# Linear attention followed by a spectral mix: the last attention step hands its weight tiles to the output phase, and y and z leave in one put

## The chip, the cores and the metric

The kernel runs on one core of one Trainium2 chip. The metric is device time in microseconds (us) from the first to the last instruction of that core. An execution of the kernel before takes 442.25 us (median of three: 441.34 to 443.05); the profiled one has a span of 441.4 us.

## The reference, cut to what matters

Shapes: q, k, v are 8 x 8 x 576 x 64 (batch, heads, sequence, head size), w_r and w_i are 64 x 512 x 512 (one matrix per frequency mode), w_ch is 512 x 512.

```python
def phi(x):
    proj = np.einsum('bhsd,df->bhsf', x, w_phi)
    proj = proj - np.max(np.abs(proj), axis=-1, keepdims=True)
    return np.concatenate([np.exp(proj), np.exp(-proj)], axis=-1)
q_p, k_p = phi(q), phi(k)
kv = np.einsum('bhsf,bhsd->bhfd', k_p, v);  z = np.sum(k_p, axis=2)
num = np.einsum('bhsf,bhfd->bhsd', q_p, kv)
den = np.einsum('bhsf,bhf->bhs', q_p, z)[..., None] + 1e-06
x = (num / den)                       # laid out as batch x sequence x 512
...
X = np.fft.rfft(x, axis=1)            # 64 lowest modes are mixed
Yr = Xr @ w_r - Xi @ w_i;  Yi = Xr @ w_i + Xi @ w_r      # per mode
y = np.fft.irfft(Y, n=S, axis=1)
u = x + y
out = u + np.maximum(u @ w_ch, 0.0)
```

The weights w_r and w_i are 134 MB in f32 and are read once. They are cast to bf16 on the way into SBUF.

## The kernel before, in words

**Two phases.** The attention phase works through 16 units (`Unit`, L101): one unit is a pair of heads (g, 4 of them) and a pair of batches (bp, 4 of them). A software pipeline (L504 to L573) runs steps n = -2 to 16; in each step one unit is finished (P: its x goes through the forward transform, `freq` and `keep_x`), one is in its second half (Q), one in its first (K), one is turned (R). In the last step, n = 16, there is only P, the last unit. The output phase (from L574) turns x into the result.

**The spectral mix.** The 64 modes form 8 octets (o = 0 to 7); each octet of a head pair g has a tile of w_r (even number) and one of w_i (odd number): key (g, 2 o + i). A tile is 1 MB in bf16, 8 KB on each of 128 partitions. `mix` (L461) takes one tile: eight matmuls into a PSUM bank `py`; after the second tile of an octet the bank is added to `yacc` (g < 3) or, for g = 3, becomes y of that octet. The keys are mixed in a fixed order (L351 to L354): all of g = 0 and 1, then g = 2 and 3 for octets 0 to 5, then octets 6 and 7 for g = 2 and 3 in turn. So (2,11) is the last of g = 2 for octet 5, (3,11) the tile that completes octet 5 over all g, and (3,15) the last of all.

**Loads.** `next_w` (L359) issues the next tile load from GpSimd's queue; one is issued after each mix. Tiles lie in nine buffers of pool `pw` (L83); six tiles of g = 0 lie in memory that is needed only later (`home`, L327; their keys are in `held`, L496). A load into a buffer waits until the tile before it in that buffer has been mixed.

**Who mixes when.** In the attention phase `some(n)` (L488) mixes up to n tiles at three or four places of a step: X = 3 a step from step 5 on (L506), also in step 16. The rest, 21 tiles, is mixed in the output phase's loop (L900). Instructions keep the order in which they are written on each engine (`InOrder`, L27).

**The output phase.** `todo` (L793) is a list of 76 tasks that are independent of the mixes that are still to come. The first 37 work on 36 chunks of x, 128 rows each: turn the chunk on TensorE, copy (VectorE), multiply with w_ch, keep the product in `xw` (ScalarE). The last three of these hold their product in PSUM. The other 39 tasks (`Absorb`, L724) add the inverse transform of octets 0 to 5 (for batches 0 and 1 also octet 6) to x and to xw: they read `yall` and `zall`, where z = y times w_ch. 42 tasks (A = 9 + K with K = 33, L795) are kept for the end: the three holds and the absorbs. In the loop, `n` tasks follow each mix (`fill`, L797); n is worked out from the number of mixes left (L912).

**y and z.** After the second tile of an octet with g = 3 (L913 to L953), y is rounded to `yst` (VectorE), turned, multiplied with w_ch (eight matmuls, 256 wide), and the product is rounded to `zst`. `yst` and `zst` have 128 partitions (mode, real or imaginary, batch) x 512; `put` (L802) stores each with a DMA from SyncE into 16 partitions of `yall` or `zall`, batch by batch in the free dimension: 128 packets of 1 KB, 128 KB. yall, zall and yl (late octets) are tiles of pool `pw`, so they take three of the nine tile buffers. Octets 6 and 7 also go to `yl`.

**The end.** After the last mix, 20 `Last` items (L811, L895 to L982) add the late octets, apply the relu and store.

Of the kernel before, what the change touches and what calls it, by code (L numbers as in the profile page):

```python
# [11 lines left out]
BF16 = mybir.dt.bfloat16  # L12
# [5 lines left out]
B_, H_, S_, D_ = 8, 8, 576, 64  # L18
NMODES = 64
DMODEL = 512  # L20
# [23 lines left out]
def kernel(  # L44
# [15 lines left out]
    pool, sp = InOrder(tc, nc.gpsimd), InOrder(tc, nc.sync)  # L60

    const = ctx.enter_context(tc.tile_pool(name="const", bufs=1))
    pers = ctx.enter_context(tc.tile_pool(name="pers", bufs=1))
# [13 lines left out]
    xflat = pers.tile([128, 16 + NG * NP * 18 * D_], BF16, name="xs")  # L77
    xs = xflat[:, 16:].rearrange("p (g b n d) -> p g b n d", g=NG, b=NP, n=18)
    yacc = pers.tile([128, NO, DMODEL], F32, name="yacc")

    XTb = [pers.tile([128, 2, 2, 2, 2, B_, 32], BF16, name=f"XT{i}") for i in range(2)]

    pw_cm = tc.tile_pool(name="pw", bufs=9)  # L83
    pw = pw_cm.__enter__()
    pin_cm = tc.tile_pool(name="pin", bufs=2)
    pin = pin_cm.__enter__()
# [14 lines left out]
    class Unit:  # L101
# [43 lines left out]
        def rows(self, tT, i, out):  # L145
# [7 lines left out]
            else:  # L153
# [3 lines left out]
            src = ps.rearrange("p (a c) f -> p a c f", a=2) if len(out.shape) == 3 else ps  # L157
            dve.tensor_reduce(out=out, in_=src, axis=AX.X, op=ALU.max,
                              apply_absolute_value=True)
# [167 lines left out]
    def home(g, w):  # L327

        if g == 0 and w in (0, 9):
            h = w // 9  # L330
            t = yacc.bitcast(BF16).rearrange("p o e -> p (o e)")[:, 4096 * h:4096 * h + 4096]
        elif g == 0 and w == 5:
            t = XTb[1].rearrange("p u r t x b m -> p (u r t x b m)")
        elif g == 0 and w in (3, 12, 13):
            t = xs[:, max(w - 10, 1)].rearrange("p b n d -> p (b n d)")[:, 0:4096]
        else:
            return pw.tile([128, 4, 2, DMODEL], BF16, name="wt", tag="wt")
        return t.rearrange("p (m r e) -> p m r e", m=4, r=2)
# [12 lines left out]
    wq = [(g, mg) for g in range(2) for mg in range(2 * NO)]  # L351
    wq += [(g, mg) for g in (2, 3) for mg in range(12)]
    wq += [(g, 2 * o + i) for o in (6, 7) for g in (2, 3) for i in range(2)]
    order = list(wq)  # L354
    wq.remove((0, 5))
    wq.insert(1, (0, 5))
    mixq = []

    def next_w(n):  # L359
        for _ in range(n):  # L360
            if wq:
                key = wq.pop(0)
                wts[key] = wload(*key)
# [65 lines left out]
    for t in range(3):  # L429
# [7 lines left out]
                      in_=every[:, 0:16].rearrange("p (a j c) -> p a c j", a=2, j=4),  # L437
                      axis=AX.X, op=ALU.add)
    dve.tensor_scalar_mul(out=minus[:, 0:4], in0=mf[0:96, 32:36], scalar1=-1.0)
# [48 lines left out]
    def some(n):  # L488
        for _ in range(n):
            if mixq:  # L490
                key = mixq.pop(0)
                mix(*key, wts.pop(key), XTb[key[0] % 2], lambda: one([128, DMODEL]))
                if key not in held:
                    next_w(1)

    held = [(0, mg) for mg in (0, 3, 5, 9, 12, 13)]  # L496
    units[1].load_k()
    units[1].load_v()
    units[1].load_q()
# [1 line left out]
    def unit(i):  # L501
        return units[i] if 0 <= i < len(units) else None

    for n in range(-2, len(units) + 1):  # L504
        P, Q, K, R = (unit(n + i) for i in (-1, 0, 1, 2))
        X = 0 if n < 4 else 6 if n == 4 else 3  # L506
        if Q:
            Q.exp_q(0)
        if K:
            K.rows_k(0)  # L510
            K.exp_k(0)
        if Q:
            Q.weigh_v2()
            if unit(n + 2):
                unit(n + 2).load_v()
        if P:
            P.freq()
            P.keep_x()
            if P.bp == NP - 1:
                mixq += [key for key in order if key[0] == P.g and (P.g < 2 or key[1] < 12)]  # L520
        if Q:
            Q.cols_q(1)
            Q.exp_q(1)
        some(1 if X else 0)
        if K:
            K.rows_k(1)
            K.exp_k(1)
        if Q:
            Q.kv()
        some(2 if n == 4 else 0)  # L530
        if K:
            K.rows_q(0)
            K.rows_k(2)
            K.rows_q(2)
            K.rows_q(1)
        if Q:
            Q.cols_q(2)
            Q.keep_kv()
            Q.exp_q(2)
        if K:  # L540
            K.exp_k(2)
            K.weigh_v()
        some(1 if X else 0)
        if R:
            R.turn_k(0)
        if K:
            K.shift_q()
        if R:
            R.turn_k(1)
        if Q:  # L550
            Q.num(0)
        if K:
            K.cols_q(0)
        if R and unit(n + 4):
            unit(n + 4).load_k()
        if Q:
            Q.num(6)
        if R:
            R.turn_q(0)
            R.turn_q(1)  # L560
            if unit(n + 4):
                unit(n + 4).load_q()
        if Q:
            Q.num(12)
        some(X - 2)
        if n == -1:
            forward_table()
        if n < 3:
            next_w((2, 3, 2, 3, 2)[n + 2])
        elif n == 3:  # L570
            next_w(1)
        if n == 6:
            pool.dma_start(wchb, moe_w_ch.rearrange("(dc p) e -> p dc e", p=128))  # L573
# [14 lines left out]
    pb_cm = tc.tile_pool(name="pb", bufs=2)  # L588
    pb = pb_cm.__enter__()
    xw = pb.tile([128, NP, 9, DMODEL], BF16, name="xw", bufs=1)  # L590
    zall = pw.tile([128, B_, DMODEL], BF16, name="zall", tag="wt")
    yall = pw.tile([128, B_, DMODEL], BF16, name="yall", tag="wt")
    yl = pw.tile([128, B_, DMODEL], BF16, name="yl", tag="wt")
    CI = pb.tile([128, 5, 128], BF16, name="CI", bufs=1)
    CL = pb.tile([128, 5, 128], BF16, name="CL", bufs=1)
# [83 lines left out]
    class Channels:  # L679
# [29 lines left out]
        def hold(self, pf):  # L709
            for g in range(NG):  # L710
                pe.matmul(pf, lhsT=self.xT[:, g, :], rhs=wchb[:, g, :],
                          start=(g == 0), stop=False)
# [80 lines left out]
    todo = [ch[0].turn] + [lambda i=i: hold(i) for i in range(len(ch))]  # L793
    todo += [c.only_x for c in ab[K:]] + [c.only_w for c in ab[K:]] + [c.all for c in full]
    A = 3 * 3 + K  # L795
# [3 lines left out]
            if todo:  # L799
                todo.pop(0)()  # L800

    def put(src, o, dst, copies):  # L802
        if o < 7:
            sp.dma_start(dst[16 * o:16 * o + 16], src)
        if o > 5:
            for s in copies:
                r = 32 * s + 16 * (o - 6)
                (pool if o == 6 else sp).dma_start(yl[r:r + 16], src)
# [91 lines left out]
    while mixq:  # L900
        key = mixq.pop(0)
        g, o, i = key[0], key[1] // 2, key[1] % 2
        if key not in wts:
            next_w(1)
        if not mixq:
            assert not todo
            seq[0].base(1)
            seq[0].base(0)
        mix(*key, wts.pop(key), XTb[g % 2], bank)
        next_w(1)  # L910
        left = len(mixq)
        n = -(-max(len(todo) - A, 0) // (left - 7)) if left > 7 else math.ceil(len(todo) / (left - 0.4)) if left else 0  # L912
        if g == NG - 1 and i == 1:  # L913
            end = left == 0
            if end:
                seq[1].base(1)
            py = pys.pop(o)
            yst = pb.tile([128, DMODEL], BF16, name="yst")
            pt = [bank([128, 2, 128], BF16) for h in range(2)]
            yT = [pb.tile([128, 2, 128], BF16, name=f"yT{h}") for h in range(2)]  # L920
            for h in range(2):
                dve.tensor_tensor(out=yst[:, H * h:H * h + H], in0=py[:, H * h:H * h + H],
                                  in1=yacc[:, o, H * h:H * h + H], op=ALU.add)
            put(yst, o, yall, (0, 2))
            if o < 5:
                fill(min(n, 1))
            for h in range(2):
                for dc in range(2):
                    pe.transpose(pt[h][:, dc, :],
                                 yst[:, H * h + 128 * dc:H * h + 128 * dc + 128], ident_b)  # L930
                if h:
                    dve.tensor_copy(yT[h], pt[h])
                else:
                    act.copy(yT[h], pt[h])
            if o < 5:
                fill(min(n - 1, 1))
            elif end:
                seq[0].straight(0)
                seq[0].keep_p()
                seq[1].base(0)  # L940
            pz = [bank([128, H]) for e in range(2)]
            for h in range(2):
                for e in range(2):
                    for dc in range(2):
                        pe.matmul(
                            pz[e], lhsT=yT[h][:, dc, :],
                            rhs=wchb[:, 2 * h + dc, H * e:H * e + H],
                            start=(h == dc == 0), stop=(h == dc == 1))
            zst = pb.tile([128, DMODEL], BF16, name="zst")
            act.copy(zst[:, 0:H], pz[0])  # L950
            dve.tensor_copy(zst[:, H:], pz[1])
            put(zst, o, zall, (1, 3))
            fill(max(n - 2, 0) if o < 5 else n)  # L953
        else:
            fill(n)
# [58 lines left out]
```

## Time and profile before

| what | from the profile of before |
|---|---|
| span | 441.4 us |
| TensorE (PE) busy | 330.6 us, 75% |
| VectorE (DVE) busy | 298.0 us, 68% |
| ScalarE (ACT) busy | 278.3 us, 63% |
| GpSimd (POOL) busy | 97.2 us, 22% |
| load queue q0 | 86.45 MB, its packets fill 99.6% of 16 engines' span |
| store queue q1 (SyncE) | 12.45 MB, 8.0% |
| weight loads on GpSimd's queue | 1024 KB each, 28.7 and 28.8 us from issue to landing (median) |
| puts into yall and zall | 7 each, 128 KB, 6.5 and 6.4 us from issue to landing (median) |
| granted TensorE clock, mean | 0.90 |

The profile's page has the busy time of each engine, then the span in 40 slices of 11 us each with the busy share in tenths (9 is 90% or more) and the DMA engines' share beside it. The chain of waits is followed back from the last instruction: each line is a start, a duration and what it was. A timeline line has start, duration, engine, line of the kernel, operation, the tiles written and read, a shape and a count, and in brackets the idle time just before it with what ended it. Nearly all instructions carry line L37, that of the helper that keeps the order, so one goes by tile names: `pt` and `one` are PSUM banks, `wt` a weight tile, `XT` the transformed x, `xs` is x, `xT` a turned chunk. "wt,XT" is a mix, "ident_b,xs" the turn of a chunk, "wchb,xT" its product with w_ch.

### The profile page before, as it was taken

The page shows a single profiled execution, that of the slowest core. Times are in us where ns is not written, and L with a number is a line of the kernel's source. Part 1 is how long each engine was busy: PE and PEld are TensorE (multiplying, and loading weights), DVE is VectorE, ACT ScalarE, POOL GpSimd, SP SyncE. Part 2 cuts the span into 40 slices and gives each one's busy share as a digit, 9 for nine tenths or more (in the row PEclk, how much of TensorE's full clock was granted, in tenths as well). Part 3 has the DMA queues.
Part 4 walks back from the last instruction along what each step waited for, and adds up shares of the span by engine and source line. Part 5 has one row for each costly group of instructions (what it writes and reads, how often), then busy time and mean ns, then how long its engine had stood idle before and what let it go on. Part 6 is the DMA issues. An engine that isn't in the chain of part 4 may idle for free.

```text
span 441.4 us, 10119 instructions
## 1 busy us (share of the span) xinstructions
PE 330.6 (75%) x4203; PEld 201.8 (46%) x4247; DVE 298.0 (68%) x583; ACT 278.3 (63%) x478; POOL 97.2 (22%) x138
## 2 busy tenths in 40 slices
PE   2577658768777787787786785926689979999992
PEld 2355546536555555455555453603345534344320
DVE  5768776776684777875877678717764333776694
ACT  3688877877797577865877766502644431656781
POOL 7232132132221222221122121211101220010171
PEclk9769987999899699885989799967999998999997
DMA  8999999999999999999999999999999999995787
GB/s 164 237 211 210 237 212 237 235 214 242 233 211 238 223 230 232 237 216 233 232 216 235 208 236 231 219 212 211 211 216 223 221 224 215 213 218 127 243 354 305
DMA packets 51582, 99.55 MB, mean 226 GB/s; under 512 B 2512, under 2 KB 13648, under 8 KB 51536
## 3 DMA queue, kind: packets, MB, share of 16 engines
q0 software_dynamic: 45376, 86.45, 99.6%
q1 hardware_dynamic: 6160, 12.45, 8.0%
q8 instruction: 33, 0.54, 0.5%
q14 instruction: 13, 0.11, 0.1%
HBM read 163.64 MB, written 9.44 MB: 392 GB/s over the span
## 4 chain that ended last, share of the span: by engine, by line
DMA 39%; PE 30%; DVE 12%; ACT 9%; issue 7%; POOL 0%; ACTq 0%; POOLq 0%; DVEq 0%
DMA vn<-in_v_dram 18%; PE one L37 11%; DMA wt<-in_moe_w_r_dram 9%; PE pt L37 9%; DMA wt<-in_moe_w_i_dram 6%; ACT AB L37 5%; PE pp L37 5%; PE two L37 5%; DMA kb<-in_k_dram 5%; DVE mk L37 3%; DVE m L37 2%; DVE xs L37 2%; DMA qb<-in_q_dram 2%; ACT AQ L37 1%; DVE va L37 1%
## 5 line engine op out<-in xcount | busy, mean ns | idle before, releaser
L37 ACT ACTIVATE AB<-two 128x1024 bf16<-128x1024 f32 x64 | 62.0, 1026 | 18.3 <-DVE mk L37 14.6
L37 ACT ACTIVATE AQ<-two 128x1024 bf16<-128x1024 f32 x64 | 62.6, 1045 | 2.6 <-PE two L37 2.5
L37 ACT CAST xw<-pt 128x512 bf16<-128x512 f32 x50 | 29.4, 588 | 46.3 <-PE pt L37 30.6
L37 DVE TENSOR_REDUCE m<-two 128x8 f32<-128x1024 f32 x32 | 39.2, 1224 | 15.3 <-PE two L37 15.2
L37 DVE TENSOR_TENSOR va<-vn,ee 128x1152 bf16<-128x1152 f32 x32 | 42.0, 1355 | 6.6 <-DMA vn<-in_v_dram 6.6
L37 DVE TENSOR_REDUCE mk<-two 128x8 f32<-128x1024 f32 x32 | 38.9, 1218 | 7.5 <-PE two L37 7.5
L37 PE MATMUL pt<-wchb,xT 128*128 128x512 bf16 x127 | 35.1, 389 | 8.1 <-DVE xT L37 6.3
L37 POOL DMA_DIRECT2D wt<-in_moe_w_i_dram x28 | 20.9, 748 | 87.2 <-PE pt L37 39.6
L37 POOL DMA_DIRECT2D wt<-in_moe_w_r_dram x30 | 22.4, 747 | 75.0 <-PE one L37 35.2
L37 PE MATMUL one<-wt,XT 128*32 128x512 bf16 x304 | 27.8, 451 | 13.9 <-DMA wt<-in_moe_w_i_dram 5.6
L37 PEld LDWEIGHTS <-xs 128*128 128x128 bf16 x624 | 31.6, 103 | 13.1 <-issue 8.0
L37 PE MATMUL two<-w2blk,qT 128*128 128x256 bf16 x128 | 22.8, 309 | 18.2 <-ACT AB L37 9.7
L37 ACT COPY qT<-one 128x512 bf16<-128x512 bf16 (+1 forms) x32 | 19.3, 641 | 26.2 <-PE one L37 25.8
L37 PEld LDWEIGHTS <-qT 128*128 128x128 bf16 x144 | 14.8, 107 | 36.6 <-issue 32.8
L37 PEld LDWEIGHTS <-XT 128*32 128x32 bf16 x512 | 14.4, 149 | 33.9 <-issue 18.8
L37 PE MATMUL two<-mT,minus 96*128 96x512 bf16 x64 | 27.1, 424 | 3.5 <-issue 1.5
L37 DVE TENSOR_TENSOR xs<-one,rd 128x384 bf16<-128x384 f32 x48 | 26.7, 557 | 1.6
L37 PEld LDWEIGHTS <-AQ 128*128 128x128 bf16 x512 | 24.2, 107 | 7.7 <-issue 3.9
L37 PE MATMUL one<-kvz,AQ 128*128 128x65 bf16 x512 | 26.9, 207 | 1.1 <-ACT qT L37 1.0
L37 DVE RECIPROCAL rd<-one 128x6 f32<-128x6 f32 x48 | 9.4, 195 | 26.7 <-PE one L37 26.6
L37 PE MATMUL two<-w2blk,kT 128*128 128x256 bf16 x128 | 20.9, 291 | 8.1 <-ACT AB L37 8.1
L37 PE MATMUL one<-va,AB 64*128 64x65 bf16 x1024 | 22.9, 199 | 4.1 <-DVE va L37 4.0
(147 smaller groups left out, 699.6 us busy)
## 6 DMA issues: line engine op xcount, KB each, us to landing
wt<-in_moe_w_r_dram POOLq DMA_DIRECT2D x30, 1024.0 KB, 28.7
wt<-in_moe_w_i_dram POOLq DMA_DIRECT2D x28, 1024.0 KB, 28.8
vn<-in_v_dram POOLq DMA_DIRECT2D x15, 576.0 KB, 25.0
out_dram<-of SPq DMA_DIRECT2D x16, 512.0 KB, 4.6
kb<-in_k_dram POOLq DMA_DIRECT2D x16, 288.0 KB, 21.8
qb<-in_q_dram POOLq DMA_DIRECT2D x16, 288.0 KB, 21.1
xs<-in_moe_w_i_dram POOLq DMA_DIRECT2D x2, 1024.0 KB, 24.8
yacc<-in_moe_w_r_dram POOLq DMA_DIRECT2D x1, 1024.0 KB, 9.6
```

What stands on the lines that cost most here:

```text
L37: ins = f(*args, **kwargs)
```

## The change

It has two halves. First, the last attention step (n = 16, where there is no Q) no longer mixes: its three tiles are left to the output phase's loop, which now has 24 mixes, with tasks between them. Second, `yst` and `zst` become two halves of one tile `st`, and one put stores both, as 2 KB packets, into one buffer `yz` in which y and z of a batch stand side by side; so octets 0 to 6 have one put each, after z. `yz` is a fixed 16 KB per partition, paid for by two of the nine tile buffers; until its first put, it serves as the home of two tiles at a time, those that would have been in buffers eight and nine (`apart_w`), up to the tiles of g = 2.

The pacing changes with it: 4 more tasks are kept (A + 4), the formula aims at one mix earlier (left > 8), and exactly four tasks follow mix (3,11) (left == 8), between the put of octet 5 and the first task that reads it.

```diff
+    yz = pers.tile([128, 2 * B_ * DMODEL], BF16, name="yz")
...
-    pw_cm = tc.tile_pool(name="pw", bufs=9)
+    pw_cm = tc.tile_pool(name="pw", bufs=7)
...
+        elif (g, w) in apart_w:
+            h = apart_w.index((g, w)) % 2
+            t = yz[:, 4096 * h:4096 * h + 4096]
...
+    held = [(0, mg) for mg in (0, 3, 5, 9, 12, 13)]
+    apart_w = [key for i, key in enumerate(k for k in wq if k not in held) if i % 9 > 6]
+    apart_w = [key for key in apart_w if order.index(key) < order.index((3, 0))]
...
-        X = 0 if n < 4 else 6 if n == 4 else 3
+        X = 0 if n < 4 or not Q else 6 if n == 4 else 3
...
-    zall = pw.tile([128, B_, DMODEL], BF16, name="zall", tag="wt")
-    yall = pw.tile([128, B_, DMODEL], BF16, name="yall", tag="wt")
+    both = yz.rearrange("p (b t e) -> p b t e", b=B_, t=2)
+    yall, zall = both[:, :, 0], both[:, :, 1]
...
-    def put(src, o, dst, copies):
-        if o < 7:
-            sp.dma_start(dst[16 * o:16 * o + 16], src)
+    def put(src, o, copies):
...
-        n = -(-max(len(todo) - A, 0) // (left - 7)) if left > 7 else math.ceil(len(todo) / (left - 0.4)) if left else 0
+        if left > 8:
+            n = -(-max(len(todo) - A - 4, 0) // (left - 8))
+        else:
+            n = 4 if left == 8 else math.ceil(len(todo) / (left - 0.4)) if left else 0
...
-            yst = pb.tile([128, DMODEL], BF16, name="yst")
+            st = pb.tile([128, 2, DMODEL], BF16, name="st")
+            yst, zst = st[:, 0], st[:, 1]
...
-            put(yst, o, yall, (0, 2))
+            put(yst, o, (0, 2))
...
-            zst = pb.tile([128, DMODEL], BF16, name="zst")
             act.copy(zst[:, 0:H], pz[0])
             dve.tensor_copy(zst[:, H:], pz[1])
-            put(zst, o, zall, (1, 3))
+            if o < 7:
+                sp.dma_start(both[16 * o:16 * o + 16], st)
+            put(zst, o, (1, 3))
```

More of the change, by code (lines that the diff above doesn't have):

```diff
@@ L494, in some @@
                     next_w(1)
-    held = [(0, mg) for mg in (0, 3, 5, 9, 12, 13)]
     units[1].load_k()
```

## The prediction

> **What bounds the kernel now.** I read the page first, then the chain of waits in order of time, then TensorE's timeline around the places that the chain names. The page says which resource never rests:
>
> ```profile
> PE 330.6 (75%) x4203; PEld 201.8 (46%) x4247; DVE 298.0 (68%) x583; ACT 278.3 (63%) x478; POOL 97.2 (22%) x138
> DMA  8999999999999999999999999999999999995787
> q0 software_dynamic: 45376, 86.45, 99.6%
> ```
>
> The load queue (q0: all weights, k, q, v) keeps the 16 DMA engines full for 36 of 40 slices, to about 404 us. No compute engine is above 75%. The last weight tile can't come earlier unless the stream has less to carry. The chain then shows where the stream hands over to TensorE:
>
> ```profile
> 284.96 38.60 DMA wt<-in_moe_w_r_dram
> ...
> 333.95 28.17 DMA wt<-in_moe_w_i_dram
> 362.12 0.04 issue
> 362.17 0.69 PE pt L37 x8
> ```
>
> Up to 362.12 the chain is loads; from 362.17 to 434.8 it is almost all TensorE, and the rest to 441.4 is the last store. The load that ends the first stretch is that of tile (3,11), the last of octet 5. TensorE's timeline shows both sides of the hand-over:
>
> ```profile
> 286.53 0.66 PE L37 MATMUL one<-wt,XT 128*32 128x512 bf16 x8
> 288.94 0.94 PE L37 MATMUL one<-wt,XT 128*32 128x512 bf16 x8 [1.75 <-DMA wt<-in_moe_w_i_dram]
> 293.85 1.09 PE L37 MATMUL one<-wt,XT 128*32 128x512 bf16 x8 [3.98 <-DMA wt<-in_moe_w_r_dram]
> 298.80 1.08 PE L37 MATMUL one<-wt,XT 128*32 128x512 bf16 x8 [3.86 <-DMA wt<-in_moe_w_i_dram]
> ...
> 358.50 0.40 PE L37 MATMUL pt<-ident_b,xs 128*128 128x128 bf16 x4
> 358.74 1.03 PE L37 MATMUL pt<-wchb,xT 128*128 128x512 bf16 x4
> 359.60 0.39 PE L37 MATMUL pt<-ident_b,xs 128*128 128x128 bf16 x4
> 359.82 1.03 PE L37 MATMUL pt<-wchb,xT 128*128 128x512 bf16 x4
> 362.17 0.66 PE L37 MATMUL pt<-wt,XT 128*32 128x512 bf16 x8 [1.31 <-DMA wt<-in_moe_w_i_dram]
> 363.36 0.62 PE L37 MATMUL pt<-ident_b,yst 128*128 128x128 bf16 x4 [0.53 <-DVE yst L37]
> 364.16 1.80 PE L37 MATMUL pt<-wchb,yT 128*128 128x256 bf16 x8 [0.19 <-ACT yT L37]
> ```
>
> From 286.5 to 298.8 it stands still for 1.75 + 3.98 + 3.86 = 9.6 us, while tiles (2,8) to (2,11) come 4.95 us apart; the change moves the mixes of the first three of them. At 362.17 it has caught up again and waits 1.31 us. After that it is behind the loads: the landing events have the eight remaining loads at 367.5, 373.4, 378.3, 383.2, 388.3, 394.4, 399.0 and 404.1, the timeline their mixes at 369.0, 374.5, 379.2, 384.9, 392.3, 397.3, 401.9 and 405.2. So two things set the end: when (3,11) lands, and how much TensorE does after it.
>
> **What the skill says.** The Trainium skill, "TensorE: Matmul & The Clock Gate", section "What's actually happening": TensorE's clock is halved after an idle window of about 3.4 us and comes back after about 3.4 us of work. The trace agrees: granted clock 0.5 from 289.20 to 302.85, and again from 364.29 to 367.70, after the waits of 1.31, 0.53 and 0.19 us. The second one costs half of 3.41, 1.7 us, on the path that sets the end (eight 256-wide matmuls take 1.80 us there, 1.04 at full clock). "DMA: Bandwidth & Descriptors", section "Queues, rings and completion order": each DMA engine takes turns between queues, packet by packet. The trace agrees: a 128 KB put of y or z lands 6.3 to 7.6 us after its issue while the loads run (yl puts in the quiet tail: from 3.3 us), and the loads slow down. Same page, "Why small descriptors are slow (HBM only)": copies within SBUF do not suffer from small descriptors, so 1 KB to 2 KB packets may bring less than the packet count suggests; no row of before has the merged put.
>
> **Part 1, three mixes move to the output phase.** The instructions stay the same in number; one mix is eight matmuls, 0.66 us. What they gain is that channel tasks (turn a chunk, multiply it with w_ch: 0.24 + 0.86 = 1.10 us by the starts 358.50, 358.74, 359.60) now stand between them. The 9.6 us of waiting get filled. But that doesn't bring (3,11) earlier: TensorE already waits for that load. The work up to there is 15 mixes of 0.66, 30 tasks of 1.10 and 5 z-products of about 1.1 us, some 48 us in the 75 us from 286.5 to 361; so TensorE will wait about 1.5 us at nearly every tile, and the gain is spent as waits. The table arithmetic on VectorE (17.1 us busy of 300 to 320), which holds up the turns, lies in the same slack. Worth: 0.
>
> **Part 2, the pacing.** There are 76 tasks and 42 of them are kept for the last mixes. Before, 21 mixes were left at the start of the output phase: 3 tasks after each of 8, then 2 after each of 5, so 2 follow (3,11). After, 24 are left: 2 after each of 15, then 4 fixed ones after (3,11). 42 remain at (2,12) in both. So two more tasks lie behind the load of (3,11), where TensorE is the path: +2 x 1.10 = +2.2 us. Their VectorE and ScalarE parts (one copy each, 0.59 us on ScalarE) lie beside it.
>
> **Part 3, one put per octet.** Ten puts before (3,11) become five. From 323.57 to 362.12 (seven loads) a load takes 5.51 us against 4.95 without puts: 7 x 0.56 = 3.9 us for nine to ten puts, 0.41 each. For the merged one: the trace's hardware-queue packets of 1,024 B take 59 ns (median), those of 2,048 B 84 ns, though most of the latter are stores. By these, 0.82 us per octet becomes 0.58, 1.2 us over five; by bytes alone only completion packets go, about 0.1 per octet (estimate), 0.5 us. I take 0.85: (3,11) lands at 361.3. -0.85 us.
>
> **Part 4, the added wait.** y now leaves only with z. y of octet 5 was put at 363.66, 1.5 us after (3,11), and z at 366.55, 4.4 after. The first absorb reads y at 372.62, 10.45 after. In after the put goes 3.9 to 4.4 us after (3,11) (by the clock) and lands 7 to 8.3 us later: two puts issued at 328.29 and 329.03 landed by 336.63, 8.3 after the first. So 10.9 to 12.7 against a need at 10.45 + 2.2, less up to 1.7 if the clock stays full: 10.95 to 12.65. The four fixed tasks just cover it; behind it in TensorE's order stand the absorbs and with them mix (2,13). 0 to 1.7 us, I take +0.3.
>
> **Part 5, the clock at the hand-over.** Before loses 1.7 us in 364.29 to 367.70. After comes to (3,11) with a load of some 65%, sometimes already slow and soon back, sometimes full, sometimes slowed as before: 0 to 1.7 us, I take half: -0.85.
>
> **Buffers.** Nine tile buffers become seven and two halves of yz: the same nine up to (2,9), then seven where before has six once yall, zall and yl take theirs. At least five loads stay queued, so the stream doesn't dry: 0. The first put no longer waits for two tile slots (322.22 and 328.29 before): 0, nobody reads y then. From (3,15) on, both programs have the same work.
>
> **Sum.** 0 + 2.2 - 0.85 + 0.3 - 0.85 = +0.8 us on 442.25: 443.0.
>
> **Rivals.** (a) Slower: the puts save only 0.5, the clock is slowed as before, and the merged put lands late: +2.2 - 0.5 + 0.5 to 1.7, 444.5 to 445.7; a second slow window would add 1.7. For it: the sharing of the engines (6.3 to 7.6 us landings) and the clear extra work. Against it: the waits in after are short, 1 to 2 us. (b) Faster: TensorE, with fewer slow windows, draws level with the last load. That lands about 1.3 us earlier, at 402.8, and the mix starts at once where it now lags 1.2 us: at best -2.5 us, 439.8. For it: the lags are only 0.9 to 4.0 us, and some 2.7 us of idle time lies between 362 and 405. Against it: these idle times are waits for VectorE and ScalarE that stay, and 2.2 us of work come on top. (c) The end doesn't move because gains and losses cancel: my forecast.
>
> **Chances.** Forecast 0.55 (441 to 444.4), (b) 0.20 (439.8 to 441), (a) 0.25 (444.4 to 446). Faster by over 0.5% means under 440.0: most of (b) is not that far, 0.15. Slower means above 444.5: 0.22. The rest, 0.63, is the same. Range 439.9 to 445.7.
>
> **What would show it.** Waits for wt of 1 to 2 us before most mixes from 300 to 361; (3,11) landing at 360.9 to 361.6; four tasks after it and TensorE the chain from there; mix (3,15) near 406; yz puts landing in 7 to 8.3 us. Wrong if TensorE is level with the loads after (3,11) (then faster), if it is late at (3,11), or if the stream has gaps (then slower).

## The result, and the profile after

The changed kernel takes 448.97 us (median; 448.45 to 449.69) against 441.88 us for the kernel before, measured beside it: a ratio of 1.0158 with a 95% interval of 1.0131 to 1.0185. It is 7 us slower. The forecast was 443.0 us; the measured time lies 3.3 us above the end of its range, 445.7.

The page of the changed kernel, with the line of the store queue q1 added to those shown of before:

```profile
PE 339.4 (76%) x4203; PEld 206.2 (46%) x4247; DVE 298.7 (67%) x583; ACT 277.9 (62%) x478; POOL 97.0 (22%) x138
DMA  7999999999999999999999999999999999993788
q0 software_dynamic: 45376, 86.45, 98.9%
q1 hardware_dynamic: 5152, 12.45, 9.2%
```

The load queue is still busy to the end of its work, with the same packets and bytes. The line to stop at is q1. The kernel before has this one:

```profile
q1 hardware_dynamic: 6160, 12.45, 8.0%
```

The change took 1,008 packets away and left the bytes as they were, and the packets' time grew from 8.0% of 441.4 us to 9.2% of 447.0: summed over the packet records, by 5.9 us of all 16 engines. Fewer packets cost more.

The chain of waits, in order of time, hands over to TensorE at the same tile, (3,11), but later: at 364.97 instead of 362.12.

```profile
327.06 37.91 DMA wt<-in_moe_w_i_dram
365.01 1.11 PE pt L37 x8
367.59 4.94 PE pt L37 x29
```

TensorE's timeline shows what became of the moved mixes, and the hand-over:

```profile
286.58 0.66 PE L37 MATMUL pt<-yz,XT 128*32 128x512 bf16 x8
...
290.33 0.66 PE L37 MATMUL pt<-yz,XT 128*32 128x512 bf16 x8
...
335.82 0.89 PE L37 MATMUL pt<-wt,XT 128*32 128x512 bf16 x8 [1.98 <-DMA wt<-in_moe_w_r_dram]
...
342.25 0.66 PE L37 MATMUL pt<-wt,XT 128*32 128x512 bf16 x8 [1.85 <-DMA wt<-in_moe_w_i_dram]
...
358.32 0.66 PE L37 MATMUL pt<-wt,XT 128*32 128x512 bf16 x8 [1.83 <-DMA wt<-in_moe_w_r_dram]
...
360.24 1.03 PE L37 MATMUL pt<-wchb,xT 128*128 128x512 bf16 x4
365.01 1.08 PE L37 MATMUL pt<-wt,XT 128*32 128x512 bf16 x8 [3.75 <-DMA wt<-in_moe_w_i_dram]
366.68 0.73 PE L37 MATMUL pt<-ident_b,st 128*128 128x128 bf16 x4 [0.59 <-DVE st L37]
367.59 1.89 PE L37 MATMUL pt<-wchb,yT 128*128 128x256 bf16 x8 [0.19 <-ACT yT L37]
...
374.20 0.66 PE L37 MATMUL pt<-wt,XT 128*32 128x512 bf16 x8
...
377.84 0.60 PE L37 MATMUL pt<-yz,CI 96*128 96x512 bf16 x2
```

The early waits for loads are gone, as forecast (in their place TensorE waits 1.57 and 3.27 us for VectorE before 296 us), and from 329 us on TensorE waits 0.4 to 3.8 us for most tiles: it is ahead of the loads. It waits 3.75 us for (3,11), after which the mix takes 1.08 us and the z-product 1.89: the granted clock is 0.5 from 363.44 to 370.26, twice as long as in the profile of before. Mix (2,12) follows 9.2 us after (3,11), before 6.8 us (362.17 to this line):

```profile
368.98 0.66 PE L37 MATMUL pt<-wt,XT 128*32 128x512 bf16 x8
```

From there on TensorE stays behind the loads: the last tile, (3,15), lands at 407.0, and its mix starts 3.5 us later.

Three terms are to be told apart: the put, the clock at the hand-over, and the two more tasks. In the experiments I use one measure beside the time: the **stretch**, the time from the landing of tile (3,2) to that of (3,15), 17 loads later, in which the puts of octets 0 to 6 fall. It is 90.44 us in the kernel before and 93.99 in the changed one. Each stretch is that of one profiled execution; the nine traces in which an octet has two puts of 1 KB packets into 16 partitions have 90.3 to 90.7 us, so a difference of more than half a microsecond is clear of the scatter. The times need more care: the runs were made in five groups, and the kernel before, measured beside each, has medians of 441.0 to 441.9 us. Where it matters, the distance to the kernel before of the same group is given.

### The profile page after: what moved, and what is told of

Read it like the earlier page. It is cut to its first block, busy times and chain, and to the rows that moved or that the text cites. A ratio compares the mean times of both kernels' runs of the same rounds, so it can differ in the third digit from the quotient of the medians.

```text
span 447.0 us, 10108 instructions
## 1 busy us (share of the span) xinstructions
PE 339.4 (76%) x4203; PEld 206.2 (46%) x4247; DVE 298.7 (67%) x583; ACT 277.9 (62%) x478; POOL 97.0 (22%) x138
## 4 chain that ended last, share of the span: by engine, by line
DMA 44%; PE 29%; DVE 13%; ACT 8%; issue 5%; POOL 1%; DVEq 0%; ACTq 0%; POOLq 0%
DMA wt<-in_moe_w_r_dram 18%; PE pt L37 13%; DMA vn<-in_v_dram 11%; DMA wt<-in_moe_w_i_dram 8%; PE one L37 7%; PE pp L37 5%; DMA kb<-in_k_dram 5%; PE two L37 4%; ACT AB L37 3%; DVE mk L37 3%; DVE m L37 3%; DVE of L37 2%; DMA qb<-in_q_dram 2%; DVE xs L37 1%; ACT AQ L37 1%
## 5 line engine op out<-in xcount | busy, mean ns | idle before, releaser
L37 PE MATMUL pt<-wchb,xT 128*128 128x512 bf16 x127 | 39.0, 420 | 9.4 <-DVE xT L37 7.0
L37 POOL DMA_DIRECT2D wt<-in_moe_w_i_dram x24 | 17.9, 745 | 86.1 <-PE pt L37 50.2
L37 POOL DMA_DIRECT2D wt<-in_moe_w_r_dram x26 | 19.3, 744 | 67.3 <-PE pt L37 28.8
L37 PE MATMUL two<-mT,minus 96*128 96x512 bf16 x64 | 28.1, 439 | 3.6 <-issue 1.8
L37 PEld LDWEIGHTS <-AQ 128*128 128x128 bf16 x512 | 25.5, 110 | 8.1 <-issue 4.8
L37 PE MATMUL one<-kvz,AQ 128*128 128x65 bf16 x512 | 28.2, 212 | 1.3 <-ACT qT L37 1.1
L37 DVE COPY xT<-pt 128x512 bf16<-128x512 bf16 x36 | 17.0, 472 | 15.6 <-PE pt L37 15.5
L37 PEld LDWEIGHTS <-xT 128*128 128x128 bf16 x168 | 16.2, 108 | 22.7 <-DVE xT L37 7.5
```

The source lines that it names most:

```text
L37: ins = f(*args, **kwargs)
```

## The experiments

**Moment or packets: two puts at the place of the merged one.**

```diff
             if o < 7:
-                sp.dma_start(both[16 * o:16 * o + 16], st)
+                sp.dma_start(yall[16 * o:16 * o + 16], yst)
+                sp.dma_start(zall[16 * o:16 * o + 16], zst)
```

> The changed kernel, but y and z of an octet leave in two puts of 128 KB (1 KB packets) right after one another, at the place of the merged put; bytes and moment are the same. Theory 'packet': 2 KB packets into 16 partitions hold the DMA engines up, 1 KB packets don't; then tile (3,11) lands near 362 instead of 365.0 and the time falls from 449.0 to 445 to 446. Rival 'burst': what costs is that 256 KB go at one moment into 16 partitions, however they are cut; then (3,11) lands near 365 and the time stays at 449.

Measured: 445.38 us; (3,11) lands at 361.5 and the stretch is 90.41 us, as in the kernel before. The same bytes at the same moment, cut in two, are 3.6 us quicker (3.25 us, each against the kernel before beside it). Burst falls.

**The old order of the puts: y early, z later,** into the same yz; all else as changed.

> The changed kernel, but y is put as soon as it is there and z later, as before (two puts of 128 KB, 1 KB packets, into the same yz). Both theories of the put (packet, burst): (3,11) lands at 362 and the time is 444 to 446, of which about 2.2 us over the kernel before are the two more tasks after (3,11) and up to 1.7 the clock. Rival 'moved mixes': the three moved mixes themselves delay the stream; then (3,11) lands after 364 here too and the time stays over 447.

Measured: 445.99 us, (3,11) at 361.6, stretch 90.54 us. So the merged put costs 3.0 us of the 7 (2.6 against the kernels before beside them). The moved mixes don't delay the stream.

**Few partitions or many: the merged put into 128 partitions.**

```diff
-                sp.dma_start(both[16 * o:16 * o + 16], st)
+                far = pb.tile([128, 2, DMODEL], BF16, name="far")
+                sp.dma_start(far, st)
```

> The changed kernel, but the merged put writes its 256 KB into a spare tile of 128 partitions x 2 KB instead of 16 partitions of yz (so yz keeps old weights, and the absorbs add a wrong y and z; the work is the same). Packets stay 2 KB, the moment stays. Theory 'partitions': the jam is at the 16 partitions that are written; then (3,11) lands at 361 to 362 and the time is 444.5 to 446. Rival '2 KB copies are slow wherever they go': (3,11) near 365, 449.

Measured: 444.70 us, (3,11) at 360.8, stretch 89.43 us. Packets of 2 KB are not slow in themselves. The packet records of the trace, from 300 us to the landing of (3,11), say what differs:

```
                          data packets of the puts      4-byte completion packets
before                    1 KB, mean  58.9 ns            median  22 ns
changed, 16 partitions    2 KB, mean 151.9 ns            median 656 ns
two puts, 16 partitions   1 KB, mean  58.9 ns            median  22 ns
merged, 128 partitions    2 KB, mean  95.8 ns            median  22 ns
```

In the changed kernel a data packet takes 96 ns at the median, as when it is spread, but up to 288 ns, and the completion packet, the last one of each engine, takes 656 ns at the median. The loads run on the same 16 engines.

**The first half alone:** no mixes in step 16, all else as before.

```diff
-        X = 0 if n < 4 else 6 if n == 4 else 3
+        X = 0 if n < 4 or not Q else 6 if n == 4 else 3
```

> The kernel before with the first half alone: the last attention step mixes nothing, 24 mixes with tasks between them, pacing formula and two puts as before (two tasks after (3,11)). My account: TensorE waits for (3,11) either way, so the time is that of before, 441.9, within 1.5 us, (3,11) lands at 362. Rival 'moved mixes cost': more idle time of TensorE before (3,11) or a late load makes it slower by 2 us or more.

Measured: 443.47 us against 441.54, 1.9 us by the medians; ratio 1.0030, interval 1.0017 to 1.0044, which is 1.3 us. The stretch is 90.37 us and (3,11) lands at 361.6, no later than before. My account missed: something costs, though the loads do not come later. The single times lie in two groups, 7 from 440.7 to 442.2 and 13 from 443.0 to 444.3 us; the median falls into the upper one, and so lies above what the ratio says. The profiled one, of the upper group, shows this in TensorE's timeline:

```profile
357.63 1.03 PE L37 MATMUL pt<-wchb,xT 128*128 128x512 bf16 x4
361.63 1.08 PE L37 MATMUL pt<-wt,XT 128*32 128x512 bf16 x8 [2.98 <-DMA wt<-in_moe_w_i_dram]
363.25 0.72 PE L37 MATMUL pt<-ident_b,yst 128*128 128x128 bf16 x4 [0.54 <-DVE yst L37]
364.16 1.89 PE L37 MATMUL pt<-wchb,yT 128*128 128x256 bf16 x8 [0.19 <-ACT yT L37]
...
369.13 0.66 PE L37 MATMUL pt<-wt,XT 128*32 128x512 bf16 x8
```

It waits 2.98 us for (3,11) and the clock is then 0.5 for 6.8 us (361.1 to 367.9). That led to the next two.

**The same, with the tasks late:** nothing follows the three moved mixes, so that from (2,11) on the order is that of before.

```diff
+        if left > 20:
+            n = 0
```

> The moved mixes alone (443.5), but no tasks after the three moved mixes, so that from (2,11) on tasks and mixes follow one another as in the kernel before. Theory 'clock': the 1.3 us that the moved mixes cost come from TensorE waiting longer for (3,11), which lengthens the slow window of its clock after it from 3.4 to 6.8 us; with the old order the wait before (3,11) is 1 to 1.5 us, the slow window 3.4 us or none, and the time 441.5 to 442. Rival: the move costs by itself (buffers, banks, late loads); then 443.5 again.

Measured: 441.74 us; ratio 1.0002, interval 0.9991 to 1.0013. The profiled execution:

```profile
359.93 1.03 PE L37 MATMUL pt<-wchb,xT 128*128 128x512 bf16 x4
361.56 0.66 PE L37 MATMUL pt<-wt,XT 128*32 128x512 bf16 x8 [0.61 <-DMA wt<-in_moe_w_i_dram]
362.75 0.62 PE L37 MATMUL pt<-ident_b,yst 128*128 128x128 bf16 x4 [0.53 <-DVE yst L37]
363.56 1.05 PE L37 MATMUL pt<-wchb,yT 128*128 128x256 bf16 x8 [0.19 <-ACT yT L37]
...
366.71 0.66 PE L37 MATMUL pt<-wt,XT 128*32 128x512 bf16 x8
```

The load lands at the same time, the wait is 0.61 us and there is no slow window: mix (2,12) comes 5.15 us after (3,11), with the moved mixes alone 7.50. The 2.35 us between them are about the distance of the two groups of times (2.0 us between their medians). The moved mixes cost nothing by themselves, within 0.6 us; that TensorE has done its tasks sooner and waits longer costs.

**Work that nobody reads, in the kernel before:** seven matmuls where it waits for (3,11), three where it waits for y.

```diff
+    def warm(n):
+        idle = bank()
+        for _ in range(n):
+            pe.matmul(idle, lhsT=ident_b, rhs=wchb[:, 0, :], start=True, stop=True)
...
+        if key == (NG - 1, 11):
+            warm(7)
         mix(*key, wts.pop(key), XTb[g % 2], bank)
...
+            if o == 5:
+                warm(3)
```

> The kernel before with ten matmuls more that nobody reads: seven of 512 columns just before mix (3,11), where TensorE waits for the load, and three before y of octet 5 is turned. Theory 'clock': TensorE stays busy at the hand-over, the slow window of 364.3 to 367.7 goes, and with it up to 1.7 us: 439.8 to 441. Rival: the clock there costs nothing, or the extra matmuls cost their 0.2 us each: 441.5 to 443.

Measured: 441.27 us; ratio 0.9998 (0.9990 to 1.0006). No gain in the median. But the times now lie from 440.8 to 441.8, where the kernel before, beside it, has 440.7 to 442.6, with 10 of its 27 above all of these, and no slow window shows in the profile. So by the times about a third of the executions of the kernel before seem to have had one at this place. The one that I had read, at 443.16 us, was one that had. The median alone would not show this, since the useless matmuls also cost something here: they outlast the wait.

```profile
361.13 1.67 PE L37 MATMUL pt<-wchb,ident_b 128*128 128x512 bf16 x6
362.74 0.66 PE L37 MATMUL pt<-wt,XT 128*32 128x512 bf16 x8
```

(3,11) had landed at 361.50, so its mix starts 1.24 us late, which takes back most of the 1.7 us that a full clock is worth. (One of the seven has no record in the trace.)

**The same in the kernel with the moved mixes,** fourteen and three.

> The moved mixes alone (443.5) with seventeen matmuls more that nobody reads: fourteen of 512 columns (3.0 us) before mix (3,11), three before y of octet 5 is turned. Theory 'clock': with TensorE busy there, the slow window after (3,11) goes; 441 to 442. Rival: the 1.9 us of the moved mixes have another cause; then 443.5 or more.

Measured: 441.60 us; ratio 1.0012 (0.9995 to 1.0028), no slow window at the hand-over in the profile. Here the matmuls fill the wait and hardly outlast it:

```profile
358.40 3.19 PE L37 MATMUL pt<-wchb,ident_b 128*128 128x512 bf16 x13
361.72 0.66 PE L37 MATMUL pt<-wt,XT 128*32 128x512 bf16 x8
```

The load landed at 361.68, and mix (2,12) follows 5.20 us after (3,11), as with the late tasks. Seventeen useless matmuls take away 1.9 us by the medians, 1.5 us against the kernels before beside them; 12 of the 13 times lie below 442.6, one is 445.28 us and stays unexplained. Together with the late tasks this shows the clock as the cause of what the moved mixes cost.

The traces of all sixteen versions, one execution each, show how the wait and the slow window go together. Where TensorE waits up to 1.07 us for (3,11), no slow window follows at the hand-over (six traces). With waits of 1.31 to 1.61 us it is 3.4 us long (three traces), with 2.98 to 3.75 us it is 6.8 us long (five traces). In between lie a wait of 2.01 us with none and one of 2.96 us with 3.4 us. The wait alone doesn't decide it, but a long one makes it likely.

**Fewer of them, in the kernel before:** four and two.

> The kernel before with six matmuls more that nobody reads, four before mix (3,11) and two before y of octet 5 is turned: as in the run with ten, but hardly longer than the wait that they fill. Theory 'clock': no slow window and nearly no cost, 440.8 to 441.2, a little under the kernel before. Rival: six are too few to keep the clock, or most runs of the kernel before have no slow window anyway; 441.3 to 441.6.

Measured: 440.92 us against 441.18; ratio 0.9991, interval 0.9983 to 0.9999, and no slow window at the hand-over in the profile, though mix (3,11) starts 0.99 us after its load. Of the versions that do all the work it is the one that is ahead of both kernels, by a quarter of a microsecond, and only just clear of the noise.

**Two tasks after (3,11) instead of four,** y early as above.

```diff
-            n = -(-max(len(todo) - A - 4, 0) // (left - 8))
+            n = -(-max(len(todo) - A - 2, 0) // (left - 8))
         else:
-            n = 4 if left == 8 else ...
+            n = 2 if left == 8 else ...
```

> The changed kernel with y put early and z later (1 KB packets, as in the run with y early) and two tasks after (3,11) instead of four (two more are spread before it). Theory: the two tasks cost 2.2 us, so 443.5, like the moved mixes alone. Rival: they lie beside waits and cost nothing; then 446 as with four tasks.

Measured: 443.94 us, against 445.99 with four: 2.05 us for two tasks, 1.8 against the kernels before beside them. With four executions of each this is known to some 1.6 us only, but the traces agree: both have the same slow window of 6.8 us, and mix (2,12) follows (3,11) after 7.71 us with two tasks and after 10.01 with four, 2.3 us apart. It is within 0.5 us (0.7 against the kernels before) of the moved mixes alone, so yz and the two tile buffers fewer cost little.

**The second half alone:** merged put and yz, but mixes and pacing as before.

> The second half of the change alone: yz, two tile buffers fewer, one merged put per octet; the last attention step mixes its three tiles and the pacing is that of before (two tasks after (3,11)). Theory: the jam of the merged put is independent of the rest; (3,11) lands 2.5 to 3.5 us later than before, near 365, and the time is 444.5 to 446.5 (up to 1.5 us more if the absorbs wait for the put of octet 5, which only two tasks cover). Rival: the jam needs the moved mixes (earlier puts); then 441.5 to 442.5.

Measured: 447.37 us against 441.33, in the upper part of what I expected, with the wait of the absorbs that I had allowed for; the four times spread from 445.5 to 448.5. The stretch is 94.26 us. (3,11) landed earlier than expected, at 362.3, since only four puts had landed by then (the fifth at 366.1). (3,15) has it all: 406.5 against 404.1 in the profile of before. And the wait that the four tasks of the change are there to cover comes out:

```profile
371.99 1.03 PE L37 MATMUL pt<-wchb,xT 128*128 128x512 bf16 x4
374.42 0.60 PE L37 MATMUL pt<-yz,CI 96*128 96x512 bf16 x2 [1.40 <-DMA yz<-st]
```

So on its own the second half costs 6.0 us, while in the change the merged put adds 3.0 to two puts. That four tasks instead of two buy back its wait would explain a part of this, but it is not shown: the profiled execution is the quickest of the four, 445.49 us, and in it the wait of 1.40 us does not reach the end, since mix (3,15) starts 0.56 us after its load again. There the later load is what counts. Why two of the four take 448.5 us is open.

**No puts for octets 0 to 6.**

> The changed kernel without the puts of octets 0 to 6 (yz keeps old weights, the absorbs add them; the other work is the same). It shows what the puts cost the stream in all. Theory: a load takes 4.95 us throughout, so (3,11) lands near 357.5 and (3,15) near 397 to 398; TensorE then bounds the end from (3,11), and the time is 440.5 to 442.5. Rival: the longer steps of the loads after 323 us have another cause than the puts; then (3,11) lands near 361 here too.

Measured: 439.34 us; loads 4.9 to 5.1 us apart but for a few pairs, (3,11) at 357.5, stretch 85.04 us. So the rival falls, and against this run all puts of the kernel before cost the stream 5.4 us, 0.77 per octet. The time is below the 440.5 to 442.5 that I expected, but falls by only 1.8 us: here TensorE, with its four tasks, bounds the end, as mix (3,15) starts 4.0 us after its load.

**How many partitions, and one DMA or two.** The merged put into 32 and into 64 partitions (`yz[r:r + 32, 0:4096]`, `far[0:64]`), and one DMA that is cut into 1 KB packets by 16 unused columns between y and z:

```diff
-            st = pb.tile([128, 2, DMODEL], BF16, name="st")
+            st = pb.tile([128, 2, DMODEL + 16], BF16, name="st")[:, :, 0:DMODEL]
```

> The changed kernel, but the merged put writes its 256 KB (2 KB packets) into 32 partitions of yz, 8 KB each, instead of 16 partitions with 16 KB (so the absorbs add wrong values; the work is the same). Theory 'the written side is full': 16 partitions take in less than the 16 DMA engines bring, 32 take twice that; then the jam is gone and (3,11) lands at 361 to 362, the time is 444.5 to 446. Rival: the jam stays until the put is spread over all partitions; then 447.5 to 449.

> The changed kernel, but the merged put writes its 256 KB (2 KB packets) into 64 partitions of a spare tile, 4 KB each (so yz keeps old weights; the work is the same). With 16 and 32 partitions the put stretched the loads by 1.3 and 1.2 us, with 128 by 0.7. Theory 'few partitions': at 64 the put's packets run near 96 ns and a put stretches the loads by 0.7 to 0.9 us. Rival 'only a full spread helps': packets stay near 140 ns and the stretch over 1.1 us.

> The changed kernel with 16 unused columns between y and z in st, so that one put still carries both, but as 256 packets of 1 KB. Theory 'packet': the cut into 2 KB packets is what holds up the engines, not that one DMA carries 256 KB; a put then stretches the loads by 0.8 us as two puts did, (3,11) lands near 361.5 and the time is 445 to 446. Rival 'one DMA of 256 KB': near 365 and 448 to 449 as with the change.

Measured, with the stretch less the 85.04 us without puts, divided by seven octets (the costs in the expectations were reckoned over two loads fewer and lie some 0.05 higher):

```
                                    us      over before   stretch   per octet
merged, 2 KB,  16 partitions      448.97       7.1         93.99      1.28
merged, 2 KB,  32 partitions      444.45       3.3         93.20      1.17
merged, 2 KB,  64 partitions      446.62       5.6         91.76      0.96
merged, 2 KB, 128 partitions      444.70       3.2         89.43      0.63
one DMA, 1 KB, 16 partitions      446.85       5.8         91.54      0.93
two DMAs, 1 KB, 16 partitions     445.38       3.8         90.41      0.77
kernel before                                              90.44      0.77
```

The time of the 32-partition run would have fitted "jam gone", but its stretch and packets (mean 137.8 ns, completion 594 ns) say that the jam is there. Its profiled execution has no slow window at the hand-over, which makes up for it, and times of 443.9 to 447.0 say that this varies. Nor is the jam gone at 64 (120.6 ns, 688 ns; times of 444.1 to 447.9), where neither of the two expectations came out. The stretch falls step by step with the partitions. It is the measure to go by in these runs, not the time: with 32 and 64 partitions the first absorb does not wait for the put of octet 5 (with 32 it starts at 373.20, and the put lands at 374.26), and each put waits for the one before it, since both write the same place.

The padded put has data packets of 61 ns on average, completion packets of 179 at the median. Of the 3.6 us of stretch by which the merged put exceeds two DMAs, it takes away 2.45: most of the cost to the stream is the cut into 2 KB packets. By the times it is 2.1 us of 3.6, or 1.3 of 3.25 against the kernels before, which four executions of each can't settle. Its remaining 1.5 us over two DMAs is explained in part: 1.1 us lie in the stretch, and the slow window at the hand-over is 6.8 us in its profile, 3.4 in that of two DMAs. Why one DMA of 1 KB packets stretches the loads more than two is open.

## Why the prediction was wrong

**What bounds the kernel: right in kind.** The stream up to (3,11), then TensorE. But this holds for an execution with a slow window. With the tasks late, where the clock after (3,11) is full, mix (2,12) starts 0.2 us after its load and (3,15) 0.3 us, with lags of up to 3.2 us only between them; there the last load sets the end again. Of each of the lags of 0.9 to 4.0 us that I read, about 1 us came from the slow window.

**Part 1, the moved mixes, worth 0: right for the stream, wrong for the time.** They take the waits for loads at 286 to 299 us away and turn them into waits later, as written, and the loads come no earlier or later. What I didn't draw from it is that the last of these waits sits just before the hand-over. It costs through part 5.

**Part 2, two more tasks, +2.2: right.** 1.8 to 2.05 us by the times, 2.3 by the traces.

**Part 3, the put, -0.85: the step that failed, and in sign.** I took packet times of 59 ns for 1 KB and 84 ns for 2 KB and multiplied; the 84 ns came from stores, which write elsewhere. In this place they took 151.9 ns on average, and the completion packets, which I had priced at about 0.1 us an octet to be saved, 656 ns at the median. I forecast (3,11) at 361.3 us, 0.85 earlier; it landed at 364.97, 3.35 us later than with y early and z later, and the time is 3.0 us longer (2.6 to 3.6, by the version with 1 KB packets that it is set against). The put itself landed 7.7 to 8.1 us after its issue, within the 7 to 8.3 of the forecast: what I had wrong is what its packets do to the loads, not how long it takes. The skill's sentence in "DMA: Bandwidth & Descriptors", section "Why small descriptors are slow (HBM only)", that copies within SBUF do not suffer from small packets, pointed the right way, and the runs agree in so far as 1 KB packets took 58.9 ns here and merging them, into the same 16 partitions, saved nothing. I used it to make the gain smaller, not to ask whether bigger packets could hurt.

**Part 4, the added wait, +0.3: nearly right.** The put of octet 5 landed at 377.72 and the first absorb started at 377.84, with no wait shown, but only 0.12 us later, in an execution whose slow clock had held TensorE up before it. How it goes at full clock with the change as it is, no trace shows. With two tasks in place of four, in the run of the second half alone, the absorb waits 1.40 us.

**Part 5, the clock, -0.85: wrong in sign.** The sum counted down from a profile that had 1.7 us of slow clock after (3,11), while the median that I added it to comes from executions of which, by the spread of the times, only about a third had it. And the wait before (3,11) got longer (2.98 us with the moved mixes alone, 3.75 in the change), where the traces have slow windows of 6.8 us. Measured: +1.9 us by the medians, +1.3 by the ratio. I also wrote that the trace agrees with an idle window of about 3.4 us before the clock is halved. It agrees with the halving and with a length of 3.41 us, not with the idle time: in the 3.41 us before 364.29 TensorE was idle for 2.05 us in all, for 1.31 at a stretch.

**Buffers, 0:** yz and two tile buffers fewer cost 0.5 to 0.7 us, within the scatter.

**How the 7.1 us are made up.** Over the kernel before beside it, the moved mixes alone take 1.9 us more, with yz 2.6, with two more tasks 4.45, with the merged put 7.1. The steps are 1.9, 0.7, 1.8 and 2.6 us (1.9, 0.5, 2.05 and 3.0 by the medians alone). Such steps add up to the whole by construction, so that they do is no proof, and the intervals leave each but the first uncertain by 1 to 2 us. What carries the account is the traces: the later landing of (3,11), the packets, the slow window, and the later (2,12) with more tasks. Of the rivals, (a) had the right side, and it named a second slow window (+1.7) but left it out of its range; the put it let save 0.5 us and never cost anything. So the range ended at 445.7.

## What to carry to other kernels

Price a merged DMA by what it does to the stream that it shares engines with, and at its own destination: the packet time of another transfer of the same size is no bound, and fewer, larger packets can be dearer. Before adding terms to a median, see whether the profiled execution is a typical one: here it lay at 443.16 us where later medians are 441.0 to 441.5, and most of the difference, by the distance of (2,12) from (3,11) 1.7 us, was the very slow window that I meant to save. Work done sooner ahead of a bound isn't free if it leaves TensorE idle just before the stretch that counts.

## What the runs showed of the hardware that was not expected

Copies of 2 KB packets from 128 partitions into few partitions of SBUF, beside a full load stream, stretch it by 1.28, 1.17, 0.96 and 0.63 us per 256 KB for 16, 32, 64 and 128 partitions. With 1 KB packets, 16 partitions cost 0.77. Where on their way the packets are held up was not measured; that 32 partitions are hardly better than 16 speaks against a limit that simply doubles with the partitions. And matmuls that nobody reads, put into a wait ahead of the bounding stretch, kept the granted clock full at the hand-over in all three profiles that have them. Ten of them cost nothing in the median, though they held mix (3,11) up by 1.24 us, and narrowed the times from 440.7 to 442.6 to 440.8 to 441.8.
